# A gated recurrence and a SoLU block on one core: the first chunk prepared in two groups, VectorE in written order, doubling one batch ahead

## The chip, the cores and the metric

The kernel runs on one core of one Trainium2 chip. The metric is the device time of one execution in microseconds. Before the change three runs took 692.04, 693.11 and 700.78 us; the median is 693.11.

## What is computed

```python
# q, k, v, a_re, a_im: (4, 8, 768, 48) = batch, heads, steps, width
mag = sqrt(a_re**2 + a_im**2)
a = (a_re + i*a_im) * minimum(mag, 0.999) / (mag + 1e-6)
for t in range(768):                       # S is complex, 48 x 48 for each batch and head
    S = a[t][:, None] * S + outer(k[t], v[t])
    y[t] = q[t] @ real(S)
x = y with the heads side by side          # (3072, 384)
h = x @ w_in                               # 384 -> 1024
z = h * softmax(h)
out = (z - mean(z)) / sqrt(var(z) + 1e-6) * g_ln @ w_out     # 1024 -> 384
```

The weights and g_ln arrive as 64-bit floating-point numbers, the others as 32-bit ones; everything on the chip is 32-bit.

## The kernel before, in words

The 768 steps are cut into 6 chunks of 128 (`ti`), and each chunk has 4 batches (`b`). That gives 24 pairs, handled one per pass of the main loop (lines 973 to 1026), with a 25th pass for what remains. Here "pass n" is the loop's n, and "part" is n modulo 4, the batch.

Pass n does three things beside one another. For its own pair it makes scores (`score`, L803, masked on VectorE in L805), the values (`values`, L815 and L818, copied out in L821) and the carried state (`carry`, L830, L833, L834). For the pair before it runs the second block (`ffn_steps`): x transposed and copied by ScalarE (L847, L850), up matmul (`up`, L855), exp on ScalarE and the product with h on VectorE (`solu`, L863, L864), z transposed (`turn_z`, L872, L873), statistics (`norm`, L885 to L891), the output matmul in two halves (`down`, L897), and, one pass later, the scaling and the store (`store`, L902, L904). For the pair after it turns the doubled k and q (`turn`, L787, copied by ScalarE in L789).

A chunk has to be prepared before its first pass (`prep_steps`). The steps are: `s0` (a maximum over a_re on VectorE, L661, which waits for the load; a clamp of a_im, L663; Ln and Exp on ScalarE, L664 and L665; a product, L666), `s1` (three VectorE steps, L671 to L673), `s2` (two squares and a Ln on ScalarE, L677 to L679, then L680 on VectorE), `s3` (Exp and Ln, L685 and L686, then L687 on VectorE), `total` for each batch (a prefix sum by matmul, L694, clamped by L695), `decay` (two Exps, L701 and L702, into the buffers of a_re and a_im, then q and k multiplied by them, L709), `ends` (the chunk's total decay, L714 to L723), `angle` (a load of the trigonometric table, arctan, and from chunk 1 on a correction of one row, L728 to L733), `phase` for each batch (a prefix sum of angles, L745 to L748), `trig` (two sines and the load of the exponential table, L755 to L757) and `doubled` (cosine and sine times k and q, 768 columns for one batch, L766). `el`, the engine of the elementwise products, is VectorE for chunk 0 and GpSimd later.

What is prepared together is a group. Before, chunk 0 is three groups: batch 0, batch 1, and batches 2 and 3. The first is prepared before the loop, then the second, and the third in passes 0 and 1, at two of the four quarter-portions a pass. Chunk 1 follows in passes 2 and 3 at the same rate. Every later chunk takes the four passes of the chunk before it, one portion each: `s0`, `s1`, `s2` in part 0; `s3`, `total`, `decay` in part 1; `ends`, `angle`, `phase` in part 2; `trig` and all eight `doubled` in part 3.

The weights are converted from 64-bit words in 14 pieces of up to 512 columns (`convert`, L612 to L628): six of w_in before the loop, eight of w_out in pass 0. One piece is two ScalarE instructions (L618, L620), four on VectorE (L622, L624, L625, L626) and two additions on GpSimd (L623, L627). The raw words come by SyncE into five buffers; the bits that are worked on have two buffers, which a piece holds until its last addition. `centre` in pass 1 scales w_out by g_ln and subtracts its mean (L632, L635, L637).

ScalarE and TensorE run their instructions in the order in which the program writes them. VectorE, GpSimd and SyncE (which issues nearly all loads and the stores) are ordered by a planner, from its own estimate of when each instruction is ready; each engine then works through its list in order. a_re, a_im, q and k have one buffer for a chunk, v has two; the doubled q has four for one batch each, the doubled k five.

Of the kernel before, what the change touches and what calls it, by code (L numbers as in the profile page):

```python
# [514 lines left out]
def whole(ctx, tc, flag, q, k, v, a_re, a_im, moe_w_in, moe_w_out, moe_g_ln, out):  # L515
# [27 lines left out]
    nat, natk = pool("f_nat", 4), pool("f_natk", 5)  # L543
    rawp = pool("f_raw", 5)
# [18 lines left out]
    groups = [(0, 0, 1), (0, 1, 2), (0, 2, B)] + [(ti, 0, B) for ti in range(1, NC)]  # L563
# [12 lines left out]
    def load(ti, names, bs=range(B)):  # L576
        for nm, src, pl in (("ar", a_re, ld), ("ai", a_im, ld), ("q", q, ld), ("k", k, ld), ("v", v, ldv)):
# [10 lines left out]
    def weight_steps():  # L588
# [22 lines left out]
        def convert(w, wide, c, f0, n):  # L611
            def f():  # L612
                raw = ahead.pop((w is w_in, c, f0), None) or fetch(w, wide, c, f0, n)
                both = zp.tile([P, 2, NW], I32, tag="zT", name="f_bits")[:, :, 0:n]
                lo, hi, x, y = raw[:, :, 0], raw[:, :, 1], both[:, 0], both[:, 1]
                ts, stt = nc.vector.tensor_scalar, nc.vector.scalar_tensor_tensor
# [6 lines left out]
                nc.gpsimd.tensor_tensor(out=x, in0=x, in1=rebias.to_broadcast([P, n]), op=OP.add)  # L623
                stt(out=x, in0=x, scalar=31, in1=x, op0=OP.arith_shift_right, op1=OP.bitwise_and)  # L624
                ts(out=hi, in0=hi, scalar1=-2 ** 31, scalar2=None, op0=OP.bitwise_and)  # L625
                stt(out=x, in0=x, scalar=3, in1=hi, op0=OP.logical_shift_left, op1=OP.bitwise_or)  # L626
                nc.gpsimd.tensor_tensor(out=w[:, c, f0:f0 + n].bitcast(I32), in0=x, in1=y, op=OP.add)  # L627
            return f  # L628

        def centre():  # L630
# [9 lines left out]
        return [convert(*s) for s in steps[:KD * (FF // NW)]], [convert(*s) for s in steps[KD * (FF // NW):]], centre, \  # L640
            lambda: [begin(*s) for s in steps[:5]]


    def prep_steps(gi):
# [4 lines left out]
        el = nc.vector if ti == 0 else nc.gpsimd  # L649
# [7 lines left out]
        def s0():  # L657
# [5 lines left out]
            el.tensor_scalar(out=ai, in0=ai, scalar1=1e15, scalar2=-1e15, op0=OP.min, op1=OP.max)  # L663
# [11 lines left out]
        def s2():  # L675
            ar, ai, x0, lr = st["ar"], st["ai"], st["x0"], st["lr"]
# [3 lines left out]
            nc.vector.scalar_tensor_tensor(out=lr, in0=ar, scalar=0.5, in1=lr, op0=OP.mult, op1=OP.add)  # L680

        def s3():

            lr, ar = st["lr"], st["ar"]
            nc.scalar.activation(out=ar, in_=lr, func=AF.Exp, scale=-1.0, bias=small)  # L685
            nc.scalar.activation(out=ar, in_=ar, func=AF.Ln, bias=unit)  # L686
            nc.vector.scalar_tensor_tensor(out=lr, in0=lr, scalar=math.log(0.999), in1=ar, op0=OP.min,  # L687
                                           op1=OP.subtract)
# [38 lines left out]
        def angle():  # L727
            nc.scalar.preload_act_table_set("trig_and_small")  # L728
# [7 lines left out]
        def phase(b):  # L736

            def f():
                if b == 0:
# [12 lines left out]
        def trig():  # L752
# [4 lines left out]
            nc.scalar.preload_act_table_set("natural_log_exp_and_others")  # L757
# [5 lines left out]
        def doubled(nm, b):  # L763
            def f():
                t = (nat if nm == "q" else natk).tile([P, H, 2, D], FP, tag=nm, name=f"f_{nm}2")
                nc.vector.tensor_tensor(  # L766
                    out=t, in0=T["cs", ti][:, b * H:(b + 1) * H],
                    in1=heads(T[nm, ti][:, b]).unsqueeze(2).to_broadcast([P, H, 2, D]), op=OP.mult
                )
                T[nm + "2", ti, b] = t  # L770
            return f


        return [
            ([s0], [], [s1, s2]),
            ([s3], [total(b) for b in bs], [decay]),
            ([], [ends], [angle] + [phase(b) for b in bs]),
            ([trig], [doubled(nm, b) for b in bs for nm in ("k", "q")], []),
        ]

# [153 lines left out]
    load(0, ("ar", "ai"), [0])  # L934
# [31 lines left out]
    for gi in range(4, NG):  # L966
        for part in range(4):
            beside[(gi - 3) * B + part] = prep[gi][part]
# [116 lines left out]
```

## Time and profile before

| | |
|---|---|
| runs | 692.04, 693.11, 700.78 us |
| profiled execution | 697.2 us |
| its span | 695.3 us |
| mean granted TensorE clock | 0.893 |
| TensorE matmuls | 519.5 us busy |
| VectorE | 341.1 us |
| ScalarE | 292.2 us |
| GpSimd | 129.4 us |

The span runs from the first to the last profiled instruction. A row of a group of instructions gives its line in the kernel, the engine (PE is TensorE, PEld its weight load, DVE VectorE, ACT ScalarE, POOL GpSimd, SP SyncE; a q behind it means the engine's queue of issues), the operation, the tile written and the tiles read, the shape and the count; behind the bar the busy time in us and the mean of one in ns; then the idle time of the engine ahead of them and what ended it. In the timeline a row begins with its start and its length in us, and the idle time ahead of it stands in brackets.

### The profile page before, as it was taken

Reading aid. Unit: us, or ns where it says so; the run is one execution under the profiler, and the core shown is the slowest. Engines: PE = TensorE matmul, PEld = TensorE weight load, DVE = VectorE, ACT = ScalarE, POOL = GpSimd, SP = SyncE. Lnnn points to the kernel's source line nnn. Section 1 sums busy time; section 2 is a strip of 40 time slices with the busy share of each in tenths; the row PEclk is TensorE's granted clock in tenths of the full one; section 3 lists DMA queues with packets and bytes.
Section 4 is the critical chain, followed back from the end, with each engine's and each line's share of the span. In section 5 each row is a group of like instructions: output and inputs, shape, how many; then the busy total and the mean of one; then the engine's idle time right before and its main releaser. Section 6 shows DMA issues by size and latency. Waiting matters only on the chain.

```text
span 695.3 us, 12935 instructions
## 1 busy us (share of the span) xinstructions
PE 519.5 (75%) x5601; PEld 334.4 (48%) x5601; DVE 341.1 (49%) x584; ACT 292.2 (42%) x445; POOL 129.4 (19%) x153
## 2 busy tenths in 40 slices
PE   0305154855848898689997888994988998899995
PEld 0104032533425565465565465663556564666652
DVE  4667776243463462573543555533635545533322
ACT  3655546126443443353542634543535535222211
POOL 0332531010401104102043002051021150000000
PEclk9998566886959899899998998998999999999999
DMA  9941207300328004125005071022080000000000
GB/s 248 196 104 40 68 15 124 44 13 0 64 40 148 2 13 81 23 57 105 12 2 103 13 126 24 13 48 56 13 149 2 13 14 13 11 13 14 13 13 19
DMA packets 132052, 35.95 MB, mean 52 GB/s; under 512 B 126992, under 2 KB 130064, under 8 KB 131984
## 3 DMA queue, kind: packets, MB, share of 16 engines
q1 hardware_dynamic: 131312, 34.62, 25.2%
q8 instruction: 46, 0.75, 0.5%
q10 hardware_dynamic: 672, 0.40, 0.2%
q14 instruction: 22, 0.18, 0.1%
HBM read 30.22 MB, written 4.72 MB: 50 GB/s over the span
## 4 chain that ended last, share of the span: by engine, by line
PE 28%; DVE 9%; ACT 6%; DMA 3%; SPq 2%; issue 1%; POOL 1%; DVEq 0%; ACTq 0%
PE f_o L897 10%; PE f_h L855 7%; PE f_turned L787 3%; PE f_score L803 2%; SPq L584 2%; DVE f_z L864 2%; DVE f_q L766 2%; PE f_d L830 1%; DMA f_ar<-in_a_re_dram 1%; PE f_phase L745 1%; DVE f_k L766 1%; PE f_L L694 1%; POOL f_ai L666 1%; DVE f_bs L885 1%; DVE f_x L733 1%
## 5 line engine op out<-in xcount | busy, mean ns | idle before, releaser
L897 PE MATMUL f_o<-f_w_out,f_zT 128*128 128x384 f32 x384 | 135.3, 505 | 0.3 <-ACT f_zT L873 0.3
L855 PE MATMUL f_h<-f_w_in,f_xT 128*128 128x512 f32 x288 | 127.7, 593 | 0.6 <-ACT f_xT L850 0.6
L897 PEld LDWEIGHTS f_o<-f_w_out,f_zT 128*128 128x128 f32 x384 | 75.6, 203 | 48.2 <-issue 6.0
L855 PEld LDWEIGHTS f_h<-f_w_in,f_xT 128*128 128x128 f32 x288 | 52.8, 190 | 58.3 <-issue 57.5
L872 PE MATMUL f_zt<-f_mats,f_z 128*128 128x128 f32 x192 | 34.1, 312 | 48.6 <-DVE f_z L864 29.5
L789 ACT COPY f_kT<-f_turned 96x512 f32<-96x512 f32 x48 | 27.9, 581 | 97.2 <-PE f_turned L787 96.8
L902 DVE TENSOR_SCALAR f_ot<-f_o,f_rs 128x384 f32<-128x384 f32 x24 | 14.8, 616 | 94.0 <-issue 49.2
L694 PE MATMUL f_L<-f_lr,f_mats 128*128 128x384 f32 x48 | 21.5, 571 | 51.6 <-DVE f_lr L687 51.5
L864 DVE TENSOR_TENSOR f_z<-f_h,f_z 128x512 f32<-128x512 f32 x48 | 32.9, 686 | 50.3 <-ACT f_z L863 50.3
L873 ACT COPY f_zT<-f_zt 128x512 f32<-128x512 f32 x48 | 27.6, 585 | 66.0 <-PE f_zt L872 65.7
L787 PE MATMUL f_turned<-f_mats,f_k 128*96 128x128 f32 x192 | 37.9, 332 | 22.9 <-DVE f_k L766 17.8
L863 ACT ACTIVATE f_z<-f_h 128x512 f32<-128x512 f32 x48 | 28.8, 600 | 53.3 <-PE f_h L855 53.2
L872 PEld LDWEIGHTS f_zt<-f_mats,f_z 128*128 128x128 f32 x192 | 22.8, 154 | 55.6 <-DVE f_z L864 38.0
L803 PE MATMUL f_score<-f_qT,f_kT 96*128 96x128 f32 x384 | 48.8, 282 | 0.0
L890 POOL TENSOR_TENSOR f_s<-f_s,f_mv 128x1 f32<-128x1 f32 x24 | 4.5, 189 | 232.1 <-DVE f_s L889 155.4
L803 PEld LDWEIGHTS f_score<-f_qT,f_kT 96*128 96x128 f32 x384 | 47.1, 200 | 0.6 <-issue 0.6
L787 PEld LDWEIGHTS f_turned<-f_mats,f_k 128*96 128x96 f32 x192 | 24.0, 148 | 38.9 <-DVE f_k L766 21.1
L850 ACT COPY f_xT<-f_xt 128x384 f32<-128x384 f32 x24 | 11.4, 477 | 72.9 <-PE f_xt L847 72.9
L745 PE MATMUL f_phase<-f_x,f_mats 128*128 128x384 f32 x48 | 26.6, 678 | 19.9 <-DVE f_x L733 12.1
L805 DVE TENSOR_TENSOR f_att<-f_score,f_mats 128x512 f32<-128x512 f32 x48 | 32.9, 690 | 14.5 <-PE f_score L803 14.5
L694 PEld LDWEIGHTS f_L<-f_lr,f_mats 128*128 128x128 f32 x48 | 8.9, 210 | 61.8 <-DVE f_lr L687 52.9
L787 PE MATMUL f_turned<-f_mats,f_q 128*96 128x128 f32 x192 | 37.1, 328 | 1.3 <-DVE f_q L766 1.3
(102 smaller groups left out, 864.3 us busy)
## 6 DMA issues: line engine op xcount, KB each, us to landing
f_ar<-in_a_re_dram SPq DMA_DIRECT2D x24, 192.0 KB, 4.2
f_ai<-in_a_im_dram SPq DMA_DIRECT2D x24, 192.0 KB, 4.7
f_q<-in_q_dram SPq DMA_DIRECT2D x24, 192.0 KB, 4.5
f_k<-in_k_dram SPq DMA_DIRECT2D x24, 192.0 KB, 4.2
f_v<-in_v_dram SPq DMA_DIRECT2D x24, 192.0 KB, 4.3
out_dram<-f_ot SPq DMA_DIRECT2D x24, 192.0 KB, 1.9
f_raw<-in_moe_w_in_dram SPq DMA_DIRECT2D x6, 512.0 KB, 7.1
f_raw<-in_moe_w_out_dram SPq DMA_DIRECT2D x8, 384.0 KB, 3.1
```

Source lines behind the costliest of these rows:

```text
L694: nc.tensor.matmul(out=ps, lhsT=tri, rhs=lm, start=True, stop=True)
L745: nc.tensor.matmul(out=ps, lhsT=turns, rhs=T["x0", ti][:, b * DM:(b + 1) * DM], start=True, stop=True)
L787: nc.tensor.transpose(out=ps[0:D2, i], in_=T[nm + "2", ti, b][:, half * 4 + i].rearrange("p u d -> p (u d)"), identity=ident)
L789: nc.scalar.copy(out=T[nm + "T", ti, b][:, half * 512:half * 512 + 512], in_=ps[0:D2].rearrange("p i t -> p (i t)"))
L803: nc.tensor.matmul(out=ps[:, i], lhsT=KT[:, x * P:(x + 1) * P], rhs=QT[:, x * P:(x + 1) * P], start=True, stop=True)
L805: nc.vector.tensor_tensor(out=st["att"][:, half * 4:half * 4 + 4], in0=ps, in1=tri.unsqueeze(1).to_broadcast([P, 4, P]), op=OP.mult)
L855: nc.tensor.matmul(out=h, lhsT=st["xT"][:, c * P:(c + 1) * P], rhs=w_in[:, c, half * 512:(half + 1) * 512], start=(c == 0), stop=(c == KD ...
L863: nc.scalar.activation(out=z, in_=h, func=AF.Exp, accum_out=sums[:, ti * B + b, half:half + 1])
L864: nc.vector.tensor_tensor(out=z, in0=h, in1=z, op=OP.mult)
L872: nc.tensor.transpose(out=ps[:, i * P:(i + 1) * P], in_=st["z"][:, c * P:(c + 1) * P], identity=ident)
L873: nc.scalar.copy(out=st["zT"][:, half * 512:(half + 1) * 512], in_=ps)
L897: nc.tensor.matmul(out=st["o"], lhsT=st["zT"][:, c * P:(c + 1) * P], rhs=w_out[:, c], start=(c == 0), stop=(c == KF - 1))
```

## The change

Chunk 0 becomes two groups of two batches, which are prepared in turn, step by step, before the loop; the first group's products run on VectorE, the second's on GpSimd, and the clamp is on GpSimd for both. `s2` loses its VectorE step to `s3`, and the last VectorE step of `s3` becomes `s4`. Each weight piece is cut into a first half `f` and a second half `g`, in the order f0, f1, g0, f2, g1 and so on; 14 of these 28 halves come before the loop, the rest in pass 0. `doubled` leaves the preparation and is done in pass n for pass n + 1. Chunk 1 is prepared in passes 0 to 3 like every other. `phase` comes after the second half of the output matmul. q and k get two buffers for a chunk, the doubled q two and the doubled k three for a batch, the raw words four. VectorE is added to the engines that run in written order.

```diff
-    nat, natk = pool("f_nat", 4), pool("f_natk", 5)
-    rawp = pool("f_raw", 5)
+    nat, natk = pool("f_nat", 2), pool("f_natk", 3)
+    rawp = pool("f_raw", 4)
...
-    groups = [(0, 0, 1), (0, 1, 2), (0, 2, B)] + [(ti, 0, B) for ti in range(1, NC)]
+    groups = [(0, 0, 2), (0, 2, B)] + [(ti, 0, B) for ti in range(1, NC)]
...
-        for nm, src, pl in (("ar", a_re, ld), ("ai", a_im, ld), ("q", q, ld), ("k", k, ld), ("v", v, ldv)):
+        for nm, src, pl in (("ar", a_re, ld), ("ai", a_im, ld), ("q", q, ldv), ("k", k, ldv), ("v", v, ldv)):
...
                 ts(out=x, in0=hi, scalar1=0x7FFFFFFF, scalar2=None, op0=OP.bitwise_and)
                 nc.gpsimd.tensor_tensor(out=x, in0=x, in1=rebias.to_broadcast([P, n]), op=OP.add)
+                ts(out=hi, in0=hi, scalar1=-2 ** 31, scalar2=None, op0=OP.bitwise_and)
+
+            def g():
+                lo, hi, x, y = st["all"]
+                stt = nc.vector.scalar_tensor_tensor
                 stt(out=x, in0=x, scalar=31, in1=x, op0=OP.arith_shift_right, op1=OP.bitwise_and)
-                ts(out=hi, in0=hi, scalar1=-2 ** 31, scalar2=None, op0=OP.bitwise_and)
                 stt(out=x, in0=x, scalar=3, in1=hi, op0=OP.logical_shift_left, op1=OP.bitwise_or)
                 nc.gpsimd.tensor_tensor(out=w[:, c, f0:f0 + n].bitcast(I32), in0=x, in1=y, op=OP.add)
...
+        pieces = [convert(*s) for s in steps]
+        order = [pieces[0][0]]
+        for this, then in zip(pieces, pieces[1:]):
+            order += [then[0], this[1]]
+        order.append(pieces[-1][1])
...
-        el = nc.vector if ti == 0 else nc.gpsimd
+        el = nc.vector if gi == 0 else nc.gpsimd
...
-            el.tensor_scalar(out=ai, in0=ai, scalar1=1e15, scalar2=-1e15, op0=OP.min, op1=OP.max)
+            nc.gpsimd.tensor_scalar(out=ai, in0=ai, scalar1=1e15, scalar2=-1e15, op0=OP.min, op1=OP.max)
...
-    load(0, ("ar", "ai"), [0])
+    load(0, ("ar", "ai"))
...
+    load(0, ("q", "k"), [0, 1])
+    weights, centre, begin_weights = weight_steps()
     begin_weights()
+    load(0, ("v",), [0])
+    load(0, ("q", "k"), [2, 3])
+    load(0, ("v",), [1, 2, 3])
...
+    for nm in ("s0", "s1", "s2", "s3", "s4", "totals", "decay"):
+        both(nm)
+    run(weights[0:2])
+    to_trig()
+    both("angle")
+    run(weights[2:4])
+    both("phases")
+    run(weights[4:6])
+    both("trig")
+    to_exp()
+    doubled(0, 0)
     for half in range(2):
         for nm in ("k", "q"):
             turn(nm, 0, 0, half)
+    both("ends")
+    run(weights[6:14])
...
         if last_ff:
             last_ff[6]()
-        run(first)
+        if part == 0:
+            now["s0"]()
+        elif part == 1:
+            now["s3"]()
+        elif part == 2:
+            now["decay"]()
+        elif part == 3:
+            now["trig"]()
+            to_exp()
+        if nxt:
+            doubled(*nxt)
         if n > 0:
             up(0)
             solu(0)
             up(1)
-        run(middle)
+        if part == 3:
+            now["ends"]()
...
         if n == 0:
-            run(w_out_steps)
+            run(weights[14:])
+        if n == 1:
+            centre()
+        if part == 1:
+            now["s4"]()
         if n > 0:
             down(0)
             norm()
...
-        run(late)
+        if part == 0:
+            now["s1"]()
+            now["s2"]()
+        elif part == 1:
+            run(now["totals"])
+        elif part == 2:
+            to_trig()
+            now["angle"]()
         if n > 0:
             down(1)
             last_ff = ff
+        if part == 2:
+            run(now["phases"])
...
-        inner.enter_context(tc.manual_schedule(engines={mybir.EngineType.Activation, mybir.EngineType.PE}))
+        inner.enter_context(tc.manual_schedule(engines={mybir.EngineType.Activation, mybir.EngineType.PE, mybir.EngineType.DVE}))
```

More of the change, by code (lines that the diff above doesn't have):

```diff
@@ L738, in f @@
             def f():
-                if b == 0:
+                if ("cs", ti) not in T:
                     T["cs", ti] = one.tile([P, B * H, 2, D], FP, tag="cs", name="f_cs")
@@ L957, in whole @@
             turn(nm, 0, 0, half)
-    for part, wait in zip(prep[1], (w_in_steps[2:4], w_in_steps[4:6], [], [])):
-        run(sum(part, []) + wait)
-    def all_of(gi, *parts):
-        return [f for part in parts for third in prep[gi][part] for f in third]
-    beside = {0: ([], all_of(2, 0), all_of(2, 1)), 1: ([], all_of(2, 2, 3), []),
-              2: ([], all_of(3, 0), all_of(3, 1)), 3: ([], all_of(3, 2, 3), [])}
-    for gi in range(4, NG):
-        for part in range(4):
-            beside[(gi - 3) * B + part] = prep[gi][part]
+    both("ends")
+    run(weights[6:14])
     chunks = [(ti, b) for ti in range(NC) for b in range(B)]
@@ L973, in whole @@
     for n in range(N + 1):
-        first, middle, late = beside.get(n, ([], [], []))
+        nxt = chunks[n + 1] if n + 1 < N else None
+        part, now = -1, None
         if n < N:
```

81 lines of the change are left out of this document (38 added, 43 removed).

## The prediction, made blind

> **What bounds the kernel now.** I read the page first for the span, then cut the span by pass, at the first score matmul of passes 0, 1, 2, 4, 20 and 23 (first fence: stretch, length, then busy time and instructions of TensorE, its weight loads, VectorE, ScalarE, GpSimd, then granted clock, DMA share, GB/s).
>
> ```profile
> span 695.3 us, 12935 instructions
> ```
>
> ```profile
> 0.00:55.90 55.90, 10.56 (x27) 5.25 (x28) 35.47 (x71) 28.16 (x45) 17.13 (x19) 1.00 0.86 177
> 55.90:97.80 41.90, 12.56 (x152) 9.59 (x151) 30.87 (x46) 21.05 (x32) 16.81 (x16) 0.61 0.11 35
> 97.80:139.10 41.30, 30.01 (x206) 18.72 (x205) 20.00 (x38) 16.99 (x28) 3.23 (x4) 0.77 0.49 77
> 139.10:220.60 81.50, 50.12 (x386) 31.19 (x385) 38.02 (x56) 32.89 (x41) 14.32 (x15) 0.77 0.26 47
> 220.60:606.50 385.90, 336.97 (x4021) 220.25 (x4020) 190.26 (x318) 171.82 (x252) 74.20 (x90) 0.92 0.21 42
> 606.50:658.60 52.10, 51.93 (x600) 33.86 (x599) 16.21 (x34) 15.45 (x33) 2.22 (x6) 1.00 0.04 13
> 658.60:695.30 36.70, 27.36 (x223) 15.58 (x221) 10.25 (x26) 5.84 (x14) 1.48 (x4) 0.97 0.06 20
> ```
>
> Passes 20 to 22 prepare nothing: 52.1 / 3 = 17.4 us each with TensorE busy for 51.93 of 52.10. That is the floor. Passes 4 to 19 prepare a next chunk and cost 385.9 / 16 = 24.1. Passes 2 and 3 cost 40.8 each, pass 1 41.3, pass 0 41.9, and 55.9 pass before any. A look inside one group of four, parts 0 to 3:
>
> ```profile
> 415.20:438.60 23.40, 20.80 (x250) 14.19 (x249) 10.83 (x16) 12.55 (x17) 4.99 (x4) 0.85 0.19 35
> 438.60:460.20 21.60, 21.06 (x258) 13.27 (x257) 10.72 (x19) 10.99 (x15) 4.78 (x7) 1.00 0.03 11
> 460.20:494.90 34.70, 24.50 (x258) 15.55 (x257) 14.46 (x28) 10.24 (x17) 7.70 (x10) 0.85 0.26 52
> 494.90:514.60 19.70, 17.95 (x250) 12.12 (x249) 12.61 (x21) 9.18 (x14) 1.52 (x3) 1.00 0.52 91
> ```
>
> Part 1 is full, parts 0 and 2 have holes. The timeline says whose:
>
> ```profile
> 427.65 1.12 PE L872 MATMUL f_zt<-f_mats,f_z 128*128 128x128 f32 x4 [2.14 <-DVE f_z L864]
> 429.05 1.50 PE L830 MATMUL f_d<-f_v,f_k 128*32 128x48 f32 x48 [0.28 <-DVE f_xn L821]
> ...
> 452.96 0.88 PE L830 MATMUL f_d<-f_v,f_k 128*32 128x48 f32 x48 [0.53 <-DVE f_xn L821]
> ...
> 473.98 1.75 DVE L661 TENSOR_SCALAR_CACHE_REDUCE f_ar<-f_ar 128x1536 f32<-128x1536 f32 x1 [6.31 <-DMA f_ar<-in_a_re_dram]
> ...
> 476.59 1.11 PE L872 MATMUL f_zt<-f_mats,f_z 128*128 128x128 f32 x4 [6.03 <-DVE f_z L864]
> ...
> 487.26 1.66 PE L745 MATMUL f_phase<-f_x,f_mats 128*128 128x384 f32 x4 [2.74 <-DVE f_x L733]
> ```
>
> At 476.59 TensorE waits 6.03 us for a product that VectorE owes it, because the planner queued the next chunk's first preparation step ahead of that product and that step waits 6.31 us for a DMA. At 487.26 it waits 2.74 for the phases, queued between the two halves of the output matmul. So what bounds passes 4 to 19 is TensorE plus the waits that VectorE's planned order causes; what bounds everything before 220 is the chain of preparation and weight conversion.
>
> **The clock, row first.** After the 2.14 us wait the 48 carry matmuls take 1.50 us, in the undisturbed pass 0.88: a short hole is paid nearly twice, since the clock then drops (0.85 in that stretch). The Trainium skill, "TensorE: Matmul & The Clock Gate", Part 1, lets the clock fall only after an idle window of about 3.4 us. The trace differs: 2.14 was enough. By that rule the 3.4 us stall that I find below would cost at most itself, and the sum would be some 9 us lower.
>
> **Part 1 of the change, the opening.** Batches 0,1 and 2,3 are prepared in turn before the first score, at a width of 768, where before batch 0, then 1, then (inside passes 0 and 1) 2 and 3 went.
>
> ```profile
> 5.15 0.55 DVE L661 TENSOR_SCALAR_CACHE_REDUCE f_ar<-f_ar 128x384 f32<-128x384 f32 x1 [4.08 <-DMA f_ar<-in_a_re_dram]
> ...
> 94.46 2.93 PE L694 MATMUL f_L<-f_lr,f_mats 128*128 128x384 f32 x4 [21.76 <-DVE f_lr L687]
> ...
> 101.91 0.38 SPq L584 DMA_DIRECT2D f_ai<-in_a_im_dram  x1
> ...
> 109.30 1.75 DVE L661 TENSOR_SCALAR_CACHE_REDUCE f_ar<-f_ar 128x1536 f32<-128x1536 f32 x1 [0.29 <-issue]
> ```
>
> ```profile
> L666 DVE TENSOR_TENSOR f_ai<-f_ai,f_x 128x768 f32<-128x768 f32 x1 | 1.0, 959 | 1.2 <-ACT f_x L665 1.2
> L664 ACT ACTIVATE f_lr<-f_ar 128x768 f32<-128x768 f32 x1 | 0.8, 843 | 0.0
> L666 POOL TENSOR_TENSOR f_ai<-f_ai,f_x 128x1536 f32<-128x1536 f32 x5 | 17.1, 3429 | 63.8 <-ACT f_x L665 63.8
> L728 ACT ACT_TABLE_LOAD x8 | 10.3, 1283 | 0.1
> ```
>
> Eight such loads took 101.9 to 109.3, 0.92 each; the first lands at 5.15, so the imaginary part of batches 0,1 (sixth in the queue) lands at about 10. From there, with 0.96 for a VectorE step, 0.84 to 0.93 for a ScalarE one, 1.7 for group 1's GpSimd product (half of 3429 ns): group 0's product at 12, VectorE's three steps at 15.3, both groups' squares and logarithm on ScalarE at 21, exponential and logarithm at 24.7, last subtraction 25.7, four totals at 2.93 per two batches with eviction 30, two exponentials per group 32, the products with q and k on GpSimd 36. Then two weight pieces, a table load of 1.28, arctan, phases, and two more pieces in between, each of which waits for the buffer of the piece two before it (some 5 us lost in all): phases at 46.5, sines at 54, table at 55.6, turned copies and first score at 58.5. Before: 55.9. Little is lost for twice the batches.
>
> **The conversion, now on VectorE ahead of the first masks.** Ten of the fourteen weight pieces (two of w_in, eight of w_out) are still to come at the first score.
>
> ```profile
> 73.20 0.56 DVE L626 SCALAR_TENSOR_TENSOR f_bits<-f_bits,f_raw 128x384 int32<-128x384 int32 x1
> ...
> 84.15 0.34 DVE L622 TENSOR_SCALAR f_bits<-f_raw 128x384 int32<-128x384 int32 x1
> ...
> 84.57 1.07 POOL L623 TENSOR_TENSOR f_bits<-f_bits,f_rebias 128x384 int32<-128x384 int32 x1 [0.77 <-DVE f_bits L622]
> ...
> 84.89 0.98 DVE L625 TENSOR_SCALAR f_raw<-f_raw 128x384 int32<-128x384 int32 x1
> ...
> 85.61 1.10 POOL L627 TENSOR_TENSOR f_w_out<-f_bits 128x384 int32<-128x384 int32 x1
> ...
> 87.05 0.35 DVE L622 TENSOR_SCALAR f_bits<-f_raw 128x384 int32<-128x384 int32 x1
> ```
>
> Before, a w_out piece took 87.05 - 84.15 = 2.9 us. In the written order (first half of the next piece, second half of this one) with two buffers the chain is: 1.10 last addition, 0.70 first half, 1.12 second half, hops: 3.2. If VectorE stood still while GpSimd adds: 1.07 + 1.10 + 0.70 + 1.12 = 4.0. Bounds 2.9 and 4.0; I take 3.4, nearer the row; a w_in piece is wider, 512 against 384, about 4.2. So 2 x 4.2 + 8 x 3.4 + 2.8 for two halves left over = 38 us (33 to 45). L625 took 0.98 beside the addition where L622, the same form, takes 0.34. The Trainium skill, "SBUF — State Buffer", section "SBUF: two separate sides", says why: VectorE and GpSimd share a port pair as an exclusive lock. By it the 4.0 holds and the sum ends 7 us higher; the 2.9 of the row says that the lock is not met every time.
>
> VectorE thus is through with the conversion, masks, and its other 6 us of pass 0 at 57 + 38 + 6 = 101. Pass 0 ends with the first chunk-1 steps (rows below): 4.4 on VectorE, then 4.8 on ScalarE, and ScalarE's copy for pass 1 stands behind them: about 110.8. As the scores of pass 1 (2.5 us with the turn) no longer hold it up, that equals a start at 108.3 against 97.8: **10.5 us lost**.
>
> Pass 1 then needs 15 (floor without turn and scores) + 2.9 totals + about 10 for centring w_out + 2 for s4, 30 us, to 140.5. Before it ended at 139.1. Passes 2 and 3 no longer carry half a chunk each; priced like parts 2 and 3 below they take 42.3 where they took 81.5. Pass 4 starts at about 182.8 instead of 220.6: **37.8 us gained**.
>
> **Part 2, passes 4 to 19.** VectorE in written order, and one batch's doubling (1.9 us) per pass instead of eight in a row.
>
> ```profile
> L672 DVE SCALAR_TENSOR_TENSOR f_x<-f_x,f_ai 128x1536 f32<-128x1536 f32 x5 | 8.8, 1750 | 0.0
> L664 ACT ACTIVATE f_lr<-f_ar 128x1536 f32<-128x1536 f32 x5 | 7.4, 1484 | 0.0
> ```
>
> ```profile
> L864 DVE TENSOR_TENSOR f_z<-f_h,f_z 128x512 f32<-128x512 f32 x48 | 32.9, 686 | 50.3 <-ACT f_z L863 50.3
> L863 ACT ACTIVATE f_z<-f_h 128x512 f32<-128x512 f32 x48 | 28.8, 600 | 53.3 <-PE f_h L855 53.2
> ```
>
> A pass with its carry is 17.4 + 0.88 = 18.3 at full clock.
> Part 0: the first step (1.75) now stands behind two masks (0.7 each) and the store (0.6): done 5.1 after the first score. Two ScalarE steps of 1.5 follow, then the first exp, two copies, the second exp and the product: second product at 11.6, wanted at 10.4, a stall of 1.2. Total 20.2 with hops.
> Part 1: s1 (1.75 + 1.75 + 0.9) starts only after the norm, 16 into the pass, and ends at 20.2; s2 (three ScalarE steps, 4.8) ends at 25, and the copy of x that the up matmuls need waits behind it until 25.5; the scores are done at 22. **A new stall of 3.4**, with 2.3 more for the clock: 18.3 + 2.9 totals + 0.4 + 5.7 = 27.3. Before 21.6.
> Part 2: the step that waited for a DMA at 473.98 is not issued before part 0 of the next group, some 30 us later, so its loads have landed; the phases stand behind the whole output matmul (5.2), which covers table 1.28, arctan 1.5 and the fix 1.75. 18.3 + 2.9 + about 2 for the two-buffer hand-over: 23.2. Before 34.7.
> Part 3: one doubling behind the sines: 19.2. Before 19.7.
> Sum 89.9 against 99.4 in this group and 385.9 / 4 = 96.5 in the mean: 4 x 6.6 = **26 us gained**. q and k in two buffers cost no time: their loads leave when the group starts, and are read two passes later. In the last passes the doubling adds 1.9 to 16.21 / 3 = 5.4 us of VectorE under 17.4 of TensorE: nothing; if that cover went, 1.9 a pass. The tail stays at 36.7.
>
> **The sum.** 695.3 - 37.8 - 26 = 631.5. The profiled execution took 697.2, 1.9 beyond its span, and lies 4.1 above the median of 693.1. Scaled so: 629.
>
> **The rivals.**
> (a) No stall in part 1: VectorE finds time for s1 before the norm needs it, or ScalarE is through. For: the same steps leave part 1 at 21.6 today. Against: in the written order s1 is behind the norm. 4 x 5.7 = 23 less: 606, and with the conversion at its lower bound 600.
> (b) The groups gain nothing: new waits in parts 0 and 1 eat what part 2 gives. 629 + 26 = 655; with the conversion at its upper bound 662.
> (c) Slower: an in-order VectorE behind SyncE's in-order queue.
>
> ```profile
> 35.21 40.18 SPq L603 DMA_DIRECT2D f_raw<-in_moe_w_out_dram  x7
> ```
>
> ```profile
> f_raw<-in_moe_w_in_dram SPq DMA_DIRECT2D x6, 512.0 KB, 7.1
> ```
>
> SyncE has stood for 40 us among seven fetches. If ten pieces each show up to their full 7.1 us (71, against 64 gained) the time is 700; it decides once the waits of VectorE on loads exceed 64 us in all, in pass 0 or at the first step of each chunk. Against: four raw buffers and two pieces of lead, 7 us.
> (d) The order written is what the planner did anyway: then part 2 keeps its 34.7, which (b) covers; the 6.31 wait shows the orders differ.
>
> **How the numbers follow.** Forecast 0.58, with its own range 608 to 650 (conversion 33 to 45, stall of part 1 between 0 and 5.7 in two groups); (a) 0.20; (b) and (d) 0.13; (c) 0.09, half of it slower by over 2%. Range 595 to 668. 2% is about what a measurement of this kernel can tell from no change; faster by that needs under 679: 0.58 + 0.20 + 0.13 and little of (c), 0.91; same 0.04; slower 0.05.
>
> **What would show it.** Right: first score at 56 to 61; pass 4 starting at 175 to 190; part 2 near 23; in part 1 an idle of about 3 us of TensorE before the up matmuls, released by ScalarE's copy; no VectorE wait on DMA of over 2 us in part 0. Wrong: part 1 at 21 to 22 (rival a), pass 4 starting after 200, or VectorE idle on raw pieces.

## The result and the profile after

The kernel after takes 636.83 us (median of four runs, 635.03 to 637.64), the kernel before beside it 696.78 (692.04 to 700.78): a ratio of 0.9138, with a 95% interval of 0.906 to 0.9217. Forecast were 629.0 and a range of 595 to 668. Each comparison below is made against runs of the kernel before on the same chip, whose median went from 692.05 to 696.78.

The profiled execution has a span of 635.8 us. Cut at the first score matmuls of the same passes as before (0, 1, 2, 4, 20, 23):

```profile
0.00:61.20 61.20, 15.15 (x35) 7.77 (x35) 33.98 (x58) 33.93 (x45) 18.76 (x20) 0.77 0.95 175
61.20:89.90 28.70, 10.97 (x148) 9.55 (x148) 17.55 (x27) 10.45 (x14) 13.63 (x10) 0.50 0.33 79
89.90:158.40 68.50, 32.45 (x209) 18.94 (x208) 37.41 (x56) 24.45 (x38) 15.60 (x16) 0.69 0.08 24
158.40:199.90 41.50, 38.40 (x377) 23.91 (x376) 23.34 (x40) 22.17 (x33) 12.29 (x14) 1.00 0.56 106
199.90:547.20 347.30, 322.57 (x4022) 206.99 (x4021) 198.90 (x315) 170.40 (x252) 100.83 (x90) 0.97 0.24 45
547.20:599.20 52.00, 51.84 (x599) 33.74 (x598) 21.22 (x39) 15.45 (x33) 2.21 (x6) 1.00 0.04 13
599.20:635.80 36.60, 27.41 (x223) 15.64 (x221) 10.73 (x30) 5.84 (x14) 1.51 (x4) 0.93 0.06 20
```

Pass 4 starts at 199.9, 20.7 us earlier than before, and passes 4 to 19 take 38.6 less. Passes 2 and 3 lost half their length (81.5 to 41.5), pass 0 fell from 41.9 to 28.7, and pass 1 grew from 41.3 to 68.5. The last two stretches are unchanged, although VectorE now carries 5 us more in passes 20 to 22. One group of four, parts 0 to 3:

```profile
374.20:392.80 18.60, 17.85 (x249) 12.02 (x248) 13.29 (x19) 7.80 (x13) 8.18 (x4) 1.00 0.04 13
392.80:419.10 26.30, 22.61 (x257) 14.09 (x256) 13.70 (x21) 12.69 (x17) 3.46 (x4) 0.94 0.03 9
419.10:441.70 22.60, 21.37 (x258) 13.30 (x257) 13.64 (x22) 12.88 (x19) 10.93 (x12) 1.00 0.56 100
441.70:460.60 18.90, 18.23 (x250) 12.03 (x249) 9.79 (x19) 9.22 (x14) 3.03 (x4) 1.00 0.65 113
```

Part 2 fell from 34.7 to 22.6; part 1 grew from 21.6 to 26.3. TensorE's timeline has the waits that remain:

```profile
82.01 1.06 PE L799 MATMUL f_turned<-f_mats,f_k 128*96 128x128 f32 x4 [17.05 <-DVE f_k L787]
...
122.87 8.41 PE L867 MATMUL f_h<-f_w_in,f_xT 128*128 128x512 f32 x12 [30.29 <-ACT f_xT L862]
...
147.22 5.49 PE L909 MATMUL f_o<-f_w_out,f_zT 128*128 128x384 f32 x8 [3.90 <-DVE f_w_out L644]
...
155.53 2.74 PE L909 MATMUL f_o<-f_w_out,f_zT 128*128 128x384 f32 x8
```

```profile
398.45 7.11 PE L867 MATMUL f_h<-f_w_in,f_xT 128*128 128x512 f32 x12 [3.68 <-ACT f_xT L862]
...
436.99 1.53 PE L758 MATMUL f_phase<-f_x,f_mats 128*128 128x384 f32 x4 [0.21 <-DVE f_x L746]
```

In part 1 (398.45) the copy of x is late by 3.68, where 3.4 was forecast. In part 2 the phases wait 0.21 where they waited 2.74, and the wait of 6.03 is gone. The opening's two long waits, 17.05 and 30.29, are both on engines that work off weight pieces in written order. VectorE there, then ScalarE:

```profile
93.87 0.36 DVE L624 TENSOR_SCALAR f_bits<-f_raw 128x384 int32<-128x384 int32 x1 [1.10 <-POOL f_w_out L633]
94.26 0.36 DVE L626 TENSOR_SCALAR f_raw<-f_raw 128x384 int32<-128x384 int32 x1
94.54 1.18 DVE L631 SCALAR_TENSOR_TENSOR f_bits<-f_bits 128x384 int32<-128x384 int32 x1
...
97.48 0.36 DVE L624 TENSOR_SCALAR f_bits<-f_raw 128x384 int32<-128x384 int32 x1 [1.17 <-POOL f_w_out L633]
...
110.69 0.55 DVE L631 SCALAR_TENSOR_TENSOR f_bits<-f_bits 128x384 int32<-128x384 int32 x1
...
112.43 1.75 DVE L683 TENSOR_TENSOR f_x<-f_ar,f_x 128x1536 f32<-128x1536 f32 x1
```

```profile
117.67 1.48 ACT L689 ACTIVATE f_ar<-f_x 128x1536 f32<-128x1536 f32 x1 [8.05 <-DVE f_x L685]
...
122.27 0.46 ACT L862 COPY f_xT<-f_xt 128x384 f32<-128x384 f32 x1
```

A piece takes 97.48 - 93.87 = 3.6 us, and VectorE waits 1.1 us in each for the buffer that GpSimd's last addition (L633) frees. Only at 112.43 is VectorE free for s1; s2 on ScalarE follows, and behind it the copy that the up matmuls wait for.

### The profile page after: what moved, and what is told of

It reads as the page before. It is cut to its first block, busy times and chain, and to the rows that moved or that the text cites. A ratio compares the mean times of both kernels' runs of the same rounds, so it can differ in the third digit from the quotient of the medians.

```text
span 635.8 us, 12921 instructions
## 1 busy us (share of the span) xinstructions
PE 498.8 (78%) x5600; PEld 316.5 (50%) x5600; DVE 343.1 (54%) x565; ACT 282.7 (44%) x428; POOL 164.8 (26%) x159
## 4 chain that ended last, share of the span: by engine, by line
PE 58%; ACT 14%; DVE 13%; POOL 6%; issue 4%; SPq 2%; DMA 0%; DVEq 0%; ACTq 0%; POOLq 0%
PE f_h L867 18%; PE f_o L909 13%; PE f_turned L799 6%; PE f_score L815 5%; PE f_zt L884 3%; PE f_d L842 3%; PE f_y L827 2%; PE f_L L708 2%; DVE f_bits L631 2%; SPq L584 2%; PE f_phase L758 2%; PE f_y L830 2%; POOL f_rs L903 2%; ACT f_kT L801 1%; DVE f_x L746 1%
## 5 line engine op out<-in xcount | busy, mean ns | idle before, releaser
L867 PE MATMUL f_h<-f_w_in,f_xT 128*128 128x512 f32 x288 | 140.4, 641 | 45.7 <-ACT f_xT L862 45.7
L867 PEld LDWEIGHTS f_h<-f_w_in,f_xT 128*128 128x128 f32 x288 | 57.2, 206 | 112.0 <-issue 95.7
L846 POOL TENSOR_TENSOR f_state<-f_state,f_tot 96x384 f32<-96x384 f32 x16 | 19.0, 1187 | 134.9 <-DVE f_state L845 134.9
L862 ACT COPY f_xT<-f_xt 128x384 f32<-128x384 f32 x24 | 11.4, 474 | 94.6 <-PE f_xt L859 94.6
L799 PE MATMUL f_turned<-f_mats,f_k 128*96 128x128 f32 x192 | 31.8, 291 | 26.2 <-DVE f_k L787 25.5
L902 POOL TENSOR_TENSOR f_s<-f_s,f_mv 128x1 f32<-128x1 f32 x24 | 10.3, 431 | 142.3 <-DVE f_s L901 142.3
L723 POOL TENSOR_TENSOR f_q<-f_q,f_ar 128x384 f32<-128x384 f32 x22 | 29.1, 1351 | 50.6 <-ACT f_ar L715 50.6
L708 PE MATMUL f_L<-f_lr,f_mats 128*128 128x384 f32 x48 | 20.3, 554 | 25.6 <-DVE f_lr L701 25.5
L884 PE MATMUL f_zt<-f_mats,f_z 128*128 128x128 f32 x192 | 29.9, 286 | 6.0 <-DVE f_z L876 6.0
L827 PE MATMUL f_y<-f_v,f_att 128*32 128x48 f32 x1536 | 34.4, 210 | 0.0
L758 PE MATMUL f_phase<-f_x,f_mats 128*128 128x384 f32 x48 | 22.3, 582 | 15.3 <-ACT f_x L743 7.2
L827 PEld LDWEIGHTS f_y<-f_v,f_att 128*32 128x32 f32 x1536 | 30.9, 112 | 5.1 <-issue 4.9
```

Of the source, the lines that this page charges most:

```text
L708: nc.tensor.matmul(out=ps, lhsT=tri, rhs=lm, start=True, stop=True)
L723: el.tensor_tensor(out=x, in0=x, in1=t[:, o], op=OP.mult)
L758: nc.tensor.matmul(out=ps, lhsT=turns, rhs=T["x0", ti][:, b * DM:(b + 1) * DM], start=True, stop=True)
L799: nc.tensor.transpose(out=ps[0:D2, i], in_=T[nm + "2", ti, b][:, half * 4 + i].rearrange("p u d -> p (u d)"), identity=ident)
L827: nc.tensor.matmul(out=y[g:g + 32, hs], lhsT=st["att"][:, x, g:g + 32], rhs=V[:, hs], start=True, stop=(ti == 0))
L867: nc.tensor.matmul(out=h, lhsT=st["xT"][:, c * P:(c + 1) * P], rhs=w_in[:, c, half * 512:(half + 1) * 512], start=(c == 0), stop=(c == KD ...
```

## The experiments

The theory after the result: the gain is the written order's on VectorE, and the opening fell short because of the pieces' two buffers and of s1 and s2 standing behind them. The rival: the layout (two groups, all chunks alike, doubling spread) brings the gain under any order. The table has each kernel's stages from its profile (us); the texts below refer to it. A ratio is a kernel's time over that of the kernel before, and the two numbers behind it are its 95% interval.

| kernel | median (range) | first score | pass 4 at | passes 4 to 19 | span |
|---|---|---|---|---|---|
| before | 696.78 | 55.9 | 220.6 | 385.9 | 695.3 |
| after | 636.83 (635.0 to 637.6) | 61.2 | 199.9 | 347.3 | 635.8 |
| 1 after, VectorE planned | 629.38 (628.6 to 630.7) | 64.9 | 184.2 | 354.7 | 626.8 |
| 2 before, VectorE written | 695.52 (691.8 to 699.8) | 57.4 | 228.2 | 381.2 | 697.4 |
| 3 three bit buffers | 626.38 (625.4 to 626.8) | 56.6 | 189.3 | 347.1 | 624.9 |
| 4 s1 early | 611.28 (609.6 to 612.9) | 61.1 | 193.4 | 326.7 | 607.8 |
| 5 q, k single | 637.77 (635.6 to 638.1) | 61.2 | 197.6 | 350.1 | 635.5 |
| 6 eight doublings | 647.14 (646.2 to 647.9) | 61.8 | 199.8 | 356.2 | 644.4 |
| 7 s1, s2 first | 627.77 (626.8 to 629.7) | 61.4 | 190.4 | 347.1 | 626.1 |
| 8 = 3 + 4 | 599.34 (598.6 to 600.5) | 56.7 | 183.0 | 326.3 | 597.5 |
| 9 = 8 + s2 first | 597.57 (596.8 to 599.9) | 56.9 | 180.8 | 326.4 | 595.7 |
| 10 = 9, pieces late | 602.97 (599.8 to 603.5) | 58.1 | 187.0 | 326.3 | 601.3 |
| 11 = 9, pieces split | 596.57 (595.7 to 598.3) | 56.6 | 179.6 | 326.5 | 594.9 |
| 12 = 9, VectorE planned | 623.05 (621.8 to 623.9) | 64.9 | 180.7 | 352.5 | 621.8 |

### 1 and 2: layout and order apart

The kernel after without the written order of VectorE, and the kernel before with it:

```diff
-        inner.enter_context(tc.manual_schedule(engines={mybir.EngineType.Activation, mybir.EngineType.PE, mybir.EngineType.DVE}))
+        inner.enter_context(tc.manual_schedule(engines={mybir.EngineType.Activation, mybir.EngineType.PE}))
```

> The changed kernel with one part undone: VectorE is again ordered by the planner; the program is otherwise the same. My theory: in passes 4 to 19 the written order is what keeps the next chunk's first step from being queued ahead of the products of the pass, so with the planner the waits of TensorE on VectorE of several us per group of four come back: 655 to 675 us, with passes 4 to 19 at 365 us or more in place of 347. Rival: the gain comes from where the program now puts the phases, the doubling and chunk 0, and the planner's order does as well: 631 to 643 us.

> The kernel before with that one part alone: VectorE in written order, nothing else changed. My theory: the DMA wait of part 2 goes (about 6 us and its clock per group), but eight doublings in a row now stand ahead of the products in part 3, and each weight piece runs as one serial chain of about 4.4 us or more in place of 2.9 in pass 0: 670 to 705 us, that is little or nothing gained against 697. Rival: the written order is the whole gain: 637 to 650 us.

The theory of the gain fell. The planned kernel is 7.5 us faster than the changed one (ratio 0.9082, 0.9026 to 0.9137). That is below both forecasts, though near the rival's. The two ratios' intervals overlap, so the ratios alone don't order the two kernels, but the slowest run of the planned one (630.7) is below the fastest of the other (635.0), and the stages agree. The written order alone gives nothing (1.0023, 0.9983 to 1.0063), as was expected of 2. By the table the layout gains 36.4 in the opening and 31.2 in passes 4 to 19; the order on top gives 7.4 in those passes and takes 15.7 in the opening. In the planned kernel's part 2 VectorE's row of before is still there. TensorE now pays for it at the phases, whose correction (L746) VectorE does behind it:

```profile
424.39 1.75 DVE L673 TENSOR_SCALAR_CACHE_REDUCE f_ar<-f_ar 128x1536 f32<-128x1536 f32 x1 [6.98 <-DMA f_ar<-in_a_re_dram]
```

```profile
428.50 5.54 PE L758 MATMUL f_phase<-f_x,f_mats 128*128 128x384 f32 x8 [4.11 <-DVE f_x L746]
```

So the order does remove this wait, as forecast; but it brings the stall of part 1, which the planned kernel lacks, and most of the gain goes.

The layout had already taken the larger part of what the prediction gave to the order. TensorE's waits for the second block's product (f_z) in passes 4 to 19 fall from 26.4 us in the kernel before to 8.6 in the planned one, while its waits for the correction ahead of the phases stay (9.8 and 11.0). Which part of the layout does this was not tested, except for the spread of the doubling (6).

### 3: three buffers for the bits

```diff
-    xp, ffp, zp, sml = pool("f_x", 2), pool("f_ff", 2), pool("f_z", 2), pool("f_sml", 4)
+    xp, ffp, zp, sml = pool("f_x", 2), pool("f_ff", 2), pool("f_z", 3), pool("f_sml", 4)
```

> The changed kernel with three buffers in place of two for the bits under conversion (and for the transposed z, which shares them); every order is the same. My theory: the two buffers set the pace of a piece (3.6 us for w_out, 4.5 for w_in), since a first half waits for the last addition of the piece two before; with three it falls to about 3.0 and 3.7, which over ten pieces on the path is 5 to 8 us: 629 to 632 us. Rival, the port that VectorE and GpSimd share sets the pace: two additions and two two-input steps exclude one another, 1.0 + 1.0 + 0.56 + 0.56 and what the one-input steps add, so it stays at 3.5 or above: 635 to 638 us.

The time fell by 10.5, more than said (ratio 0.9028, 0.8987 to 0.9069). VectorE's timeline in this kernel:

```profile
91.35 0.35 DVE L624 TENSOR_SCALAR f_bits<-f_raw 128x384 int32<-128x384 int32 x1
91.73 1.05 DVE L626 TENSOR_SCALAR f_raw<-f_raw 128x384 int32<-128x384 int32 x1
...
94.39 0.35 DVE L624 TENSOR_SCALAR f_bits<-f_raw 128x384 int32<-128x384 int32 x1
```

A piece takes 94.39 - 91.35 = 3.04 and no wait is left: VectorE itself is now the pace, with L626 held to 1.05 beside GpSimd's addition where it took 0.36 before. The first score comes 4.6 earlier (the six halves ahead of it), the other pieces give the rest. The groups are unchanged, as they must be.

### 4: s1 ahead of the norm

```diff
         if n < N:
             values()
+        if part == 0:
+            now["s1"]()
...
         if part == 0:
-            now["s1"]()
             now["s2"]()
```

> The changed kernel with s1 (three VectorE steps of the next chunk) moved from behind the norm to behind the copy of the values, s2 on ScalarE left where it is. My theory: the 3.7 us for which TensorE waits in part 1 for ScalarE's copy of x, behind s2, behind s1, behind the norm, falls below 1, and with the clock that the hole costs part 1 goes from 26.3 to 27.5 down to about 21.8: 4 x 5 us, and 2 to 3 us at the opening, so 612 to 618 us. Rival: the wait moves to the carried state and the norm, which then stand behind 4.4 us of VectorE, and no more than 8 us are gained: 629 to 637 us.

611.28 (ratio 0.8822, 0.8767 to 0.8876), a little below what the theory said, since the move also shortens the opening by 6.5 us (s1 of pass 0 no longer stands behind the pieces). Part 1 in this kernel, as a stretch, on ScalarE and on TensorE:

```profile
376.27:397.91 21.64, 20.92 (x258) 13.50 (x257) 13.19 (x20) 10.06 (x16) 3.43 (x4) 1.00 0.03 11
```

```profile
378.42 0.46 ACT L862 COPY f_xT<-f_xt 128x384 f32<-128x384 f32 x1
```

```profile
378.93 5.42 PE L867 MATMUL f_h<-f_w_in,f_xT 128*128 128x512 f32 x12 [0.71 <-ACT f_xT L862]
```

The stall shrinks from 3.68 to 0.71, the up matmuls run at full clock (5.42 against 7.11), and the pass is 4.7 shorter (5.9 where it was 27.5). The stall in part 1 was one step's place in the list.

### 5 and 6: the buffers of q and k, and the spread of the doubling

In 5, q and k have one buffer for a chunk (pool ld for ldv). In 6, besides, all eight doublings of a chunk are done in part 3:

```diff
-    nat, natk = pool("f_nat", 2), pool("f_natk", 3)
+    nat, natk = pool("f_nat", 4), pool("f_natk", 5)
...
-        if nxt:
-            doubled(*nxt)
+        if nxt and nxt[1] == 0:
+            for j in range(B):
+                doubled(nxt[0], j)
```

> The changed kernel with one buffer instead of two for a chunk of q and of k; nothing else. My theory: the loads of q and k then leave only after the last doubling in part 2 and land some 12 us later, GpSimd's products follow them and end in part 3 before the sines do, so next to nothing is lost: 0 to 4 us, 636 to 641 us. Rival: the products come late for the doubling in part 3 and TensorE waits there in each group: 645 us or more.

> The changed kernel with the doubling undone: all eight of a chunk in a row in part 3 (for chunk 0 ahead of the loop), with the buffers for that, and one buffer for q and k to make room; VectorE stays in written order. My theory: in written order the products of part 3 stand behind some 8 to 9 us of doubling that begins only after the sines, so TensorE waits about 7 us there in each of five groups, and 2 more for its clock, and the opening gets 6 us longer: 670 to 690 us. Rival: the place of the doubling is without effect, TensorE has other work: 636 to 645 us.

The second buffer is worth nothing that can be told (0.9188, 0.9146 to 0.923). The spread, 6 against 5, is worth 9.4 (0.9331, 0.9276 to 0.9386), which fits neither theory: the wait of 7 us per group did not come. In the profiles 6.1 of it lies in passes 4 to 19, nearly all in part 3 (20.1 to 21.4 where 5 has 17.8 to 19.2), and 2.2 ahead of pass 4. The last of the eight on VectorE with the second block's product behind it, and TensorE's next step:

```profile
367.04 0.95 DVE L787 TENSOR_TENSOR f_q<-f_cs,f_q 128x768 f32<-128x768 f32 x1
367.90 0.68 DVE L876 TENSOR_TENSOR f_z<-f_h,f_z 128x512 f32<-128x512 f32 x1
```

```profile
368.74 0.63 PE L884 MATMUL f_zt<-f_mats,f_z 128*128 128x128 f32 x4 [0.67 <-DVE f_ok L728]
```

TensorE waits 0.67 (the row names the small step that ended last): until then it had the up matmuls, the turns and the values to do. What a late step costs is the wait it leaves, not its length.

### 7 to 11: what bounds the opening

7 is the kernel after with s1 and s2 of pass 0 ahead of the remaining pieces; 8 joins 3 and 4; 9 adds s2 of pass 0 ahead of the pieces; 10 and 11 move pieces:

```diff
         if n == 0:
+            now["s1"]()
+            now["s2"]()
             run(weights[14:])
...
-        if part == 0:
+        if part == 0 and n > 0:
             now["s1"]()
             now["s2"]()
```

> The kernel after, with s1 and s2 of chunk 1 written in pass 0 ahead of the eight remaining weight pieces instead of behind them; the later chunks are as in the kernel after. Theory 1: the 17 us by which pass 4 comes too late are for two thirds a matter of order: VectorE does s1 only behind the last half of a piece (112.4), ScalarE's three steps of s2 follow (117.7 to 122.3), and ScalarE's copy of x, behind them, releases the up matmuls at 122.9. With s1 and s2 ahead of the pieces the copy is next on ScalarE after the last piece's own two steps, which end at 109.6, so the up matmuls begin near 110 to 112, pass 4 starts near 188, and the time is 624 to 628. Theory 2: the pieces' own end bounds pass 1 (VectorE's last half, the centring and the output matmul stand behind it), so what ScalarE gains is waited for later: 633 to 638.

> The kernel after with both edits that gained: three buffers for the bits under conversion, and s1 of the next chunk behind the values in part 0. Theory 1: one gain is in the opening, the other in the groups, so they add: 611.3 less 10.5, that is 599 to 603. Theory 2: in pass 0 both shorten the same wait (the up matmuls of pass 1 behind the pieces), so some 6 of the 10.5 are counted twice: 605 to 609.

> As the kernel with both edits (three buffers for the bits, s1 early), and in pass 0 alone s2 also ahead of the remaining weight pieces. Theory 1: ScalarE's copy of x in pass 1 no longer stands behind the 4.6 us of s2, and its end comes some 5 to 8 us earlier: 593 to 597. Theory 2: pass 1 is bound by the end of the pieces on VectorE, so nothing changes against the kernel with both edits: 599 to 603.

The time of 7 lies in the range of theory 1 (0.903, 0.8965 to 0.9095), though each step came some 2 us later than it said (up matmuls at 114.3, pass 4 at 190.4): pass 4 is 9.5 earlier, so more than half of the 17 us was order. 8 came as theory 1 said (0.8619, 0.8559 to 0.8678): 599.34, the two gains add. 9 gave 2.2 in the opening, not 5 to 8, and its 597.57 is hardly to be told from 8 (0.8599, 0.8537 to 0.8662). ScalarE's row in 9 says why:

```profile
110.14 1.58 ACT L697 ACTIVATE f_ar<-f_lr,f_bias 128x1536 f32<-128x1536 f32 x1 [8.14 <-DVE f_lr L696]
```

The copy of x is released earlier, but now s3 waits 8.14 us on ScalarE (3.55 in 8) for its VectorE step behind the pieces, and the exponentials of the second block wait behind s3: theory 2, one step later.

```diff
-    run(weights[6:14])
...
-            run(weights[14:])
+            run(weights[6:])
```

> As the last kernel, and the eight halves of weight pieces that stood between the first turned copies and pass 0 are written into pass 0, behind its own steps, with the other halves. Theory 1: pass 0's second pair of products no longer waits on VectorE behind pieces, so pass 1's score starts 15 to 20 us earlier; but the eleven pieces then run in one row at 3.0 to 3.6 us from about 66 and end at 99 to 106, where they end now too, and pass 1's up matmuls wait for them: within 4 us of the last kernel. Theory 2: the order on VectorE is what the opening waits for, not the sum of the pieces: 10 us or more less than the last kernel. Theory 3: the first step of chunk 1 waits on VectorE for its load now that it comes earlier: slower by 5 us or more.

602.97 (0.8655, 0.859 to 0.8721), 5.4 more than 9: the size fits theory 3, its reason does not, since no row of VectorE waits for a load. TensorE:

```profile
65.26 1.06 PE L799 MATMUL f_turned<-f_mats,f_k 128*96 128x128 f32 x4 [3.42 <-DVE f_k L787]
...
107.14 8.16 PE L867 MATMUL f_h<-f_w_in,f_xT 128*128 128x512 f32 x12 [33.44 <-ACT f_xT L862]
```

The wait in pass 0 falls to 3.42, and pass 1's scores start 11.5 earlier. But the pieces no longer use the time in pass 0 when VectorE had nothing else, they end 5 us later (VectorE's last half at 112.1, in 9 at 107.0), and the up matmuls start that much later too. That fits theory 1, by which the sum of the pieces on VectorE bounds the opening; that it could cost 5 us theory 1 had not.

```diff
-            run(weights[14:])
+            run(weights[14:21])
         if n == 1:
+            run(weights[21:])
             centre()
```

> As the kernel with all three edits (three buffers for the bits, s1 early, s2 of pass 0 ahead of the pieces), with the fourteen remaining halves of weight pieces split: seven in pass 0, seven in pass 1 just ahead of the centring. Theory 1: the row of pieces on VectorE and ScalarE is the chain of the opening, but the up matmuls, the exponentials and the products of pass 1, some 17 us of it, need no w_out and stand behind it only by the written order; beside the last four pieces they are hidden in part, so pass 2 starts 5 to 10 us earlier: 587 to 593. Theory 2: VectorE has no room between its pieces, so that what goes ahead of the last ones only delays them: 596 to 600.

596.57 (0.8617, 0.8574 to 0.8661) is not to be told from 9; theory 2. The up matmuls start at 94.08 where 9 has 102.15; the last pieces then come later, and the centring waits instead, at half clock:

```profile
94.08 7.12 PE L867 MATMUL f_h<-f_w_in,f_xT 128*128 128x512 f32 x12 [9.85 <-POOL f_w_out L633]
...
115.93 8.15 PE L642 MATMUL f_mean<-f_w_out,f_mats 128*128 128x384 f32 x16 [8.59 <-ACT f_w_out L639]
```

The reason is not only theory 2's. Behind the second block the pieces run at 3.6 again, since VectorE waits for a buffer; the transposed z shares the three buffers with the bits.

```profile
110.47 0.36 DVE L624 TENSOR_SCALAR f_bits<-f_raw 128x384 int32<-128x384 int32 x1 [1.17 <-POOL f_w_out L633]
```

Whether the z of pass 1 is what takes the third buffer was not tested, and a fourth was not tried.

### 12: the order again, on the mended list

Kernel 9 with VectorE planned (the edit of 1).

> As the kernel with all three edits, with VectorE's order left to the planner. Theory 1: what the written order gives is its place in the groups of four (26.3 to 28 us less over passes 4 to 19 against the planned kernel), and that stays; the opening is no better planned once the pieces run at 3 us each: 612 to 625. Theory 2: the planner puts the pieces of the opening better, by the 13 us that it had there before, and finds s1 early by itself: 580 to 597. Between the two nothing is told.

623.05 (0.8992, 0.8949 to 0.9036), theory 1. By the table 9 and 12 reach pass 4 at 180.8 and 180.7; from there the written order gains 26.1 us. In the change as made it cost 7.5; with s1 and s2 earlier and a third buffer it is worth 25.5. Kernel 9 (or 11) is the best version found: 39 us below the kernel after.

## Why the prediction came out as it did

The forecast was 7.8 us too low. That it came so near is in part luck: two terms were off in opposite directions, each by more than the whole. Pass 4 was put at 182.8 and came at 199.9 (17.1 late), and passes 4 to 19 were put at 4 x 89.9 = 359.6 and took 347.3 (12.3 less). Of the rest, 3.5 is the step from span to median: it was scaled down by 2.5 from the three runs shown, and the median lies 1.0 above this span.

Of the five signs that it named, three came: part 2 near 23, TensorE idle in part 1 until ScalarE's copy, and no wait of VectorE for a load in part 0. Two did not: the first score came at 61.2 (56 to 61 was named) and pass 4 at 199.9 (175 to 190), only just short of the 200 that was to show it wrong.

**The opening: mechanism right, four sizes off.** The chain was the forecast one (pieces on VectorE, s1, s2 on ScalarE, the copy of x). The up matmuls of pass 1 were put at 110.8 and came at 122.87. VectorE's rows give the parts: its first piece, the masks that interrupt the pieces, and the piece behind the break.

```profile
61.38 0.68 DVE L631 SCALAR_TENSOR_TENSOR f_bits<-f_bits 128x512 int32<-128x512 int32 x1
...
78.04 1.28 DVE L817 TENSOR_TENSOR f_att<-f_score,f_mats 128x512 f32<-128x512 f32 x2
...
88.07 0.55 DVE L631 SCALAR_TENSOR_TENSOR f_bits<-f_bits 128x384 int32<-128x384 int32 x1
```

It is through with the pieces at 112.43, not 101, which is 11.4: it begins them at 61.4, not 57 (4.4, of which 2.7 is the late first score, 61.2 for 58.5); they take 41.0, not 38 (3.0; a w_out piece 3.6, not 3.4); and the break for masks, s0 and doubling is 10.0, not 6 (4.0), since VectorE waits twice for TensorE in it, 2.70 and 1.61. The last 0.6 is s1 and s2, 10.4 for 9.8. Then pass 1 needed 35.6, not 30: the up matmuls took 8.41 where a full clock gives 5.3, and the first half of the output matmul 5.49 where the second took 2.74, together 5.8. The clock was charged in part 1 and not here, behind a wait that was itself forecast.

**The pace of the pieces.** The bounds of 2.9 and 4.0 hold 3.6; the step that failed is the "3.2" of the chain, which took L631 and L632 at 1.12 together. L631 took 1.18 beside GpSimd's addition and 0.55 without, in the rows above. With a third buffer a piece takes 3.04 (experiment 3), so the other 0.6 is what the wait of 1.1 for the buffer costs, less the 0.7 by which L626 is held without it. The 4.0 that the prediction worked out by the Trainium skill's rule ("SBUF — State Buffer", section "SBUF: two separate sides") was too high, but nearer than the 2.9 of the old row.

**Part 1.** Forecast 27.3 with a stall of 3.4 and 2.3 for the clock; measured 26.3 and 27.5 by turns with 3.68 (the last section says why they alternate). The up matmuls behind the stall took 7.11 and 8.3 by turns where a full clock gives 5.32: 1.8 and 3.0 for the clock. Experiment 4 shows cause and price: without the stall 21.6. Rival (a), 606 with no stall, was what the kernel could have done, not what it did.

**Part 2 and the order: the cause misjudged.** Forecast 23.2, measured 22.6; "VectorE in written order" as the remover of the DMA wait is right for this part (the planned kernel still waits 6.98). What fell is the balance behind it: I read the gain of passes 4 to 19 as the order's, and the layout alone gives 31.2 of 38.6. The prediction priced the edit only as a whole, and never the layout under the planner.

**Parts 0 and 3.** 18.6 for 20.2 and 18.9 for 19.2: the second product was late by 0.75 and not 1.2, and the hops that I added on top were not there. Over four groups these two make 7.6 of the 12.3.

**Buffers, rivals, tail.** That q and k in two buffers cost and gain nothing held (5). Rival (c) did not occur: no row of VectorE in these passes waits for a raw piece. Rival (d) is excluded by 1 and 2. The tail stayed (36.6).

## What to carry to other kernels

Price a new layout and a new order apart, and find for each step put into a written list what stands behind it on its engine and on the next one: here one step's place was worth 25 us, as much as the whole order. A row of conversions on one engine is a bound of its own: it pays to use that engine's idle time for it, and moving the row about only moves the wait. Look for the clock behind every forecast wait, not only behind the one that is being looked at.

## What the runs showed of the hardware

A small instruction on GpSimd is held by a large one on VectorE. In the kernel after, the two 128x1 steps of the statistics run beside s1 in part 0, and without it in part 1 (GpSimd, then VectorE):

```profile
388.83 1.64 POOL L902 TENSOR_TENSOR f_s<-f_s,f_mv 128x1 f32<-128x1 f32 x1 [0.83 <-DVE f_s L901]
390.55 2.70 POOL L903 TENSOR_TENSOR f_rs<-f_s,f_bias 128x1 f32<-128x1 f32 x1
...
413.96 0.19 POOL L902 TENSOR_TENSOR f_s<-f_s,f_mv 128x1 f32<-128x1 f32 x1 [1.05 <-DVE f_s L901]
414.22 0.55 POOL L903 TENSOR_TENSOR f_rs<-f_s,f_bias 128x1 f32<-128x1 f32 x1
```

```profile
388.67 1.75 DVE L683 TENSOR_TENSOR f_x<-f_ar,f_x 128x1536 f32<-128x1536 f32 x1
390.45 1.76 DVE L684 SCALAR_TENSOR_TENSOR f_x<-f_x,f_ai 128x1536 f32<-128x1536 f32 x1
392.25 0.96 DVE L685 TENSOR_SCALAR f_x<-f_x 128x1536 f32<-128x1536 f32 x1
```

They end at 390.47 and 393.25, each just as a step of s1 does (390.42 and 393.21). Which of two starts first matters: L626 took 0.36 in the kernel after, where it started ahead of the addition (94.26, GpSimd's at 94.31), and 1.05 in experiment 3, where it started behind it (91.73, GpSimd's at 91.57). The Trainium skill, "SBUF — State Buffer", section "SBUF: two separate sides", says that of a GpSimd instruction and a VectorE one that needs the shared ports, whichever starts first keeps them for the whole instruction. L626 and the first of the two small steps agree. The second one shows more: it started at 390.55 beside L684, and when L685 followed at 392.25 it was held through that too.

The same hole is not paid alike each time. In the planned kernel TensorE waits 2.14 in part 0 of two groups; the carry matmuls behind it took 1.50 in one and 0.88 in the other:

```profile
286.20 0.66 PE L884 MATMUL f_zt<-f_mats,f_z 128*128 128x128 f32 x4 [2.14 <-DVE f_z L876]
287.60 1.50 PE L842 MATMUL f_d<-f_v,f_k 128*32 128x48 f32 x48 [0.75 <-DVE f_xn L833]
...
376.26 0.66 PE L884 MATMUL f_zt<-f_mats,f_z 128*128 128x128 f32 x4 [2.14 <-DVE f_z L876]
377.66 0.88 PE L842 MATMUL f_d<-f_v,f_k 128*32 128x48 f32 x48 [0.74 <-DVE f_xn L833]
```

The record of the granted clock in the traces shows the difference. In all fourteen traces the clock changes only at multiples of 3.41 us from one another, and what it becomes goes by how much of the stretch before the matmuls were busy. Of 1994 stretches at full clock, the 104 that were busy for under 0.43 of the time were all followed by half clock, and the 1870 busy for 0.54 or more all by full clock; between the two both occur. The two holes of 2.14 us in these stretches (length, then TensorE's busy time first, the granted clock third from the end):

```profile
283.47:286.88 3.41, 1.24 (x8) 0.77 (x8) 3.41 (x5) 0.59 (x1) 0.00 (x0) 1.00 0.00 0
286.88:290.29 3.41, 2.69 (x54) 2.53 (x55) 2.64 (x7) 0.71 (x2) 1.24 (x3) 0.50 0.02 5
...
372.21:375.62 3.41, 1.79 (x112) 1.45 (x100) 3.41 (x5) 1.48 (x4) 0.00 (x0) 1.00 0.02 5
375.62:379.03 3.41, 2.03 (x57) 1.73 (x58) 3.26 (x8) 0.59 (x1) 0.42 (x2) 1.00 0.00 0
```

The first hole lies in one stretch, which is busy for 1.24 of 3.41 us (0.36), and the next stretch runs at half clock. The second is divided between two, busy for 0.52 and 0.59, and the clock stays. The way back shows the same record: none of 261 stretches at half clock that were busy for under 0.78 was followed by full clock. So the stall of part 1 costs one stretch at half clock or two, 26.3 or 27.5 us for the pass: behind the stall at 398.45 the first stretch at half clock is busy throughout; in the group before it is busy for only 2.48 of 3.41, and a second one follows. The prediction took one such row for a rule; what a hole of 2 us costs depends on where it falls.
